# Five equal chunks become seven of two sizes in a one-queue streaming kernel (x + alpha·fx)

## Chip, cores and metric

The kernel runs on 1 core of one Trainium2 chip. The metric is the device time of one execution in microseconds (us), lower is better. The time before is 153.1 us, the median of six runs between 152.75 and 153.47.

## What is computed

```
B, S, D = 512, 32, 640          # x, fx, out: bfloat16 [512, 32, 640]; alpha: bfloat16 [1]
def reference(x, fx, alpha):
    return x + alpha * fx
```

Each of the three large arrays holds 10,485,760 elements, 20.97 MB. The kernel reads two of them and writes one, 62.92 MB in all, and does one multiply and one add for each element.

## The kernel before

The arrays are seen as 128 rows, one for each partition, of 81,920 elements (160 KiB) that lie contiguously in memory. Each row is cut into five chunks of CHUNK = 16,384 elements (32 KiB), so that a load or a store of one chunk is 128 rows of 32 KiB, 4 MiB.

There are two pools of buffers on the chip: `xs` with four buffers for chunks of x (line 54) and `fs` with two for chunks of fx (line 55). Chunk k goes through four steps:

- `load_x(k)` (line 59) and `load_f(k)` (line 63) are DMAs from memory into a buffer of each pool.
- `compute(k)` (line 69) is one instruction of the vector engine (DVE), scalar_tensor_tensor, which writes fx·alpha + x over the x buffer. For the last chunk it is cut into two halves.
- `store(k)` (line 80) is a DMA from the x buffer to the output; for the last chunk there are two, one for each half.

All of these DMAs are issued by one engine, SyncE (SP; its sequencer is SPq in the profile), into one DMA queue (q1). SP issues in the order of the program and waits ahead of an instruction whose buffer is not free or whose data is not there. The order is written by hand (`manual_schedule`, lines 85 to 105). On SP's queue, with s for a store, it reads

```
x0 f0 x1 f1 x2 | f2 s0 x3 | f3 s1 x4 | f4 s2 | s3 | s4a s4b
```

What holds back an issue is of three kinds. A load of fx into a used buffer waits until the compute that read it is done: f2 waits for compute 0, f3 for compute 1, f4 for compute 2. A load of x into a used buffer waits until the store out of it has landed: x4 waits for s0. A store waits for its compute. The 16 DMA engines of the core take the DMAs of the queue in order, eight rows of each DMA to an engine.

The scalar alpha takes a separate way (`alpha_to_lanes`, lines 16 to 27): a small DMA from the scalar engine's queue, a 1x128 matmul that copies the value to all partitions, and a copy to a_f. It is done 2.3 us into the span.

Of the kernel before, what the change touches and what calls it, by code (L numbers as in the profile page):

```python
# [1 line left out]

# [4 lines left out]

ACT = mybir.ActivationFunctionType
ALU = mybir.AluOpType
F32 = mybir.dt.float32  # L10
BF16 = mybir.dt.bfloat16

CHUNK = 16384


def alpha_to_lanes(nc, consts, psum, alpha, eng):

    P = nc.NUM_PARTITIONS
    a_1 = consts.tile([1, 1], alpha.dtype, name="a_1")
    eng.dma_start(out=a_1[:], in_=alpha[None, :])  # L20
    ones = consts.tile([1, P], alpha.dtype, name="ones")
    nc.vector.memset(ones[:], 1.0)  # L22
    a_ps = psum.tile([P, 1], F32, name="a_ps")
    nc.tensor.matmul(a_ps[:], ones[:], a_1[:], start=True, stop=True)  # L24
    a_f = consts.tile([P, 1], F32, name="a_f")
    nc.vector.tensor_copy(out=a_f[:], in_=a_ps[:])  # L26
    return a_f


@with_exitstack  # L30
def kernel(
    ctx: ExitStack,
    tc: tile.TileContext,
    x: bass.AP,
    fx: bass.AP,
    alpha: bass.AP,
    out: bass.AP,
):
    nc = tc.nc
    P = nc.NUM_PARTITIONS  # L40
    xv = x.flatten_outer_dims().rearrange("(p n) d -> p (n d)", p=P)
    fxv = fx.flatten_outer_dims().rearrange("(p n) d -> p (n d)", p=P)
    ov = out.flatten_outer_dims().rearrange("(p n) d -> p (n d)", p=P)
    F = xv.shape[1]
    K = F // CHUNK
    assert K * CHUNK == F and K == 5

    consts = ctx.enter_context(tc.tile_pool(name="consts", bufs=1))
    psum = ctx.enter_context(tc.tile_pool(name="psum", bufs=1, space=bass.MemoryType.PSUM))
    xs = ctx.enter_context(tc.tile_pool(name="xs", bufs=4))  # L50
    fs = ctx.enter_context(tc.tile_pool(name="fs", bufs=2))
    ctx.enter_context(tc.manual_schedule())

    a_f = alpha_to_lanes(nc, consts, psum, alpha, nc.scalar)
    xt, ft = {}, {}

    def load_x(k):
        xt[k] = xs.tile([P, CHUNK], x.dtype, tag="x", name="x_t")
        nc.sync.dma_start(out=xt[k][:], in_=xv[:, bass.ts(k, CHUNK)])  # L59

    def load_f(k):
        ft[k] = fs.tile([P, CHUNK], fx.dtype, tag="f", name="f_t")
        nc.sync.dma_start(out=ft[k][:], in_=fxv[:, bass.ts(k, CHUNK)])

    def compute(k, parts=1):
        n = CHUNK // parts
        for j in range(parts):
            s = bass.ts(j, n)
            nc.vector.scalar_tensor_tensor(  # L69
                out=xt[k][:, s],  # L70
                in0=ft[k][:, s],
                scalar=a_f[:],
                in1=xt[k][:, s],
                op0=ALU.mult,
                op1=ALU.add,
            )

    def store(k, j=0, parts=1):
        n = CHUNK // parts
        nc.sync.dma_start(  # L80
            out=ov[:, k * CHUNK + j * n : k * CHUNK + (j + 1) * n],
            in_=xt[k][:, bass.ts(j, n)],
        )

    load_x(0)
    load_f(0)
    load_x(1)
    load_f(1)
    load_x(2)
    compute(0)  # L90
    load_f(2)
    store(0)
    load_x(3)
    compute(1)
    load_f(3)
    store(1)
    load_x(4)
    compute(2)
    load_f(4)
    store(2)  # L100
    compute(3)
    store(3)
    compute(4, 2)
    store(4, 0, 2)
    store(4, 1, 2)


# [1 line left out]
_INS = ['x', 'fx', 'alpha']  # L109
_OUTS = [((512, 32, 640), 'bfloat16')]  # L110


# [23 lines left out]
```

## Time and profile before

| What | Value |
|---|---|
| Median of six runs | 153.1 us (152.75 to 153.47) |
| The profiled execution's own time | 153.15 us |
| Its span, first to last instruction | 151.4 us |
| DVE busy | 86.9 us (57%) in 8 instructions |
| DMA queue q1 | 62.92 MB, busy 97.6% of 16 engines' span |
| Mean DMA rate over the span | 416 GB/s |

The profile tells for each engine how long it was busy and what ended its idle time; for DMAs, when SP issued one and how long after it landed. A DMA has landed when the last of its 16 engines has posted its completion. In this execution the DMAs of q1 were issued and landed at these times (us from the span's start):

| DMA | x0 | f0 | x1 | f1 | x2 | f2 | s0 | x3 |
|---|---|---|---|---|---|---|---|---|
| issued | 0.7 | 1.2 | 1.6 | 2.1 | 2.7 | 40.3 | 40.7 | 41.1 |
| landed | 13.14 | 22.85 | 32.56 | 42.28 | 52.00 | 62.28 | 72.21 | 81.93 |

| DMA | f3 | s1 | x4 | f4 | s2 | s3 | s4a | s4b |
|---|---|---|---|---|---|---|---|---|
| issued | 59.7 | 60.1 | 72.3 | 79.7 | 80.1 | 109.4 | 130.4 | 139.1 |
| landed | 91.98 | 101.73 | 111.40 | 121.45 | 131.14 | 140.82 | 145.68 | 150.53 |

s4a and s4b are 2 MiB each (128 rows of 16 KiB), all others 4 MiB.

The trace also records each row that a DMA engine moved, as a packet with its start and duration. In this execution a row of 32 KiB took 1,213 ns in the median, and a row of 16 KiB 611 ns.

### The profile page before, as it was taken

How to read it: one execution, taken by the hardware profiler on the slowest of the kernel's cores; microseconds unless marked ns; L12 is line 12 of the kernel's file. 1: busy time of each engine (PE TensorE's matmuls, PEld its weight loads, DVE VectorE, ACT ScalarE, POOL GpSimd, SP SyncE). 2: the span in 40 equal slices, each digit the busy share in tenths (PEclk: the TensorE clock that was granted, in tenths of full speed). 3: DMA queues.
4: the chain of work that ended last, by engine and by line, in shares of the span. 5: the costliest groups of instructions: out<-in, count | busy, mean ns of one | idle time of the engine just before them, and what ended most of it. 6: DMA issues, size and time to landing. Idle time of an engine off the chain costs nothing.

```text
span 151.4 us, 85 instructions
## 1 busy us (share of the span) xinstructions
PE 0.2 (0%) x1; PEld 0.1 (0%) x1; DVE 86.9 (57%) x8; POOL 0.2 (0%) x4
## 2 busy tenths in 40 slices
PE   0000000000000000000000000000000000000000
PEld 0000000000000000000000000000000000000000
DVE  0000009999689997599990006999800089997000
POOL 0000000000000000000000000000000000000000
DMA  6999999999999999999999999999999999999993
GB/s 182 459 450 424 424 416 416 433 442 459 450 424 424 416 416 416 407 424 416 416 416 433 476 424 442 433 416 407 424 442 433 459 433 442 416 416 403 437 424 139
DMA packets 2306, 62.92 MB, mean 416 GB/s; under 512 B 258, under 2 KB 258, under 8 KB 258
## 3 DMA queue, kind: packets, MB, share of 16 engines
q1 hardware_dynamic: 2304, 62.92, 97.6%
q10 hardware_dynamic: 2, 0.00, 0.0%
HBM read 41.94 MB, written 20.97 MB: 416 GB/s over the span
## 4 chain that ended last, share of the span: by engine, by line
DMA 56%; DVE 29%; DVEq 6%; issue 0%; SPq 0%
DMA f_t<-in_fx_dram 56%; DVE x_t L69 29%; DVEq L131 6%; SPq L59 0%; DVEq L69 0%
## 5 line engine op out<-in xcount | busy, mean ns | idle before, releaser
L69 DVE SCALAR_TENSOR_TENSOR x_t<-f_t,a_f,x_t 128x16384 bf16<-128x16384 bf16 (+1 forms) x6 | 86.6, 14439 | 50.2 <-DMA f_t<-in_fx_dram 50.2
L26 DVE COPY a_f<-a_ps 128x1 f32<-128x1 f32 x1 | 0.2, 158 | 1.1 <-PE a_ps L24 1.1
L22 DVE MEMSET ones<- 1x128 bf16 x1 | 0.2, 165 | 0.8 <-PEq L120 0.8
L24 PE MATMUL a_ps<-a,ones 1*128 1x1 bf16 x1 | 0.2, 159 | 1.9 <-DMA a<-in_alpha_dram 1.9
L120 POOL MEMSET const-bfloat16-1.0<- 128x1 bf16 x1 | 0.1, 102 | 0.0
L120 POOL MEMSET const-uint8-127<- 128x1 uint8 x1 | 0.1, 102 | 0.0
L24 PEld LDWEIGHTS <-ones 1*128 1x128 bf16 x1 | 0.1, 100 | 1.0 <-DVE ones L22 1.0
L120 POOL MEMSET const-float32-1.0<- 128x1 f32 x1 | 0.1, 99 | 0.0
L120 POOL MEMSET const-float32-0.0<- 128x1 f32 x1 | 0.1, 98 | 0.2 <-issue 0.2
## 6 DMA issues: line engine op xcount, KB each, us to landing
x_t<-in_x_dram SPq DMA_DIRECT2D x5, 4096.0 KB, 35.0
f_t<-in_fx_dram SPq DMA_DIRECT2D x5, 4096.0 KB, 32.3
out_dram<-x_t SPq DMA_DIRECT2D x4, 4096.0 KB, 36.6
out_dram<-x_t SPq DMA_DIRECT2D x2, 2048.0 KB, 15.3
a<-in_alpha_dram ACTq DMA_DIRECT2D x1, 0.0 KB
```

Source lines behind the costliest of these rows:

```text
L22: nc.vector.memset(ones[:], 1.0)
L24: nc.tensor.matmul(a_ps[:], ones[:], a_1[:], start=True, stop=True)
L26: nc.vector.tensor_copy(out=a_f[:], in_=a_ps[:])
L69: nc.vector.scalar_tensor_tensor(out=xt[k][:, s], in0=ft[k][:, s], scalar=a_f[:], in1=xt[k][:, s], op0=ALU.mult, op1=ALU.add,)
L120: nc = _bacc.Bacc("TRN2", target_bir_lowering=False, num_devices=1)
L131: with _tile.TileContext(nc) as tc:
```

## The change

The five equal chunks become seven: four of 8,192 elements (16 KiB rows, 2 MiB for a load or store) and then three of 16,384 (32 KiB rows, 4 MiB). The buffers keep their number and their size of 32 KiB for each partition; a small chunk fills half of one. The last chunk is no longer cut: it is computed by one instruction and stored by one DMA. The order on SP's queue becomes

```
x0 f0 x1 f1 x2 | f2 s0 x3 | f3 s1 x4 | f4 s2 x5 | f5 s3 x6 | f6 s4 | s5 | s6
```

The waits are of the same kinds: f2 to f6 wait for computes 0 to 4, and x4, x5, x6 wait for the landing of s0, s1, s2. There are 21 DMAs on q1 in place of 16 and seven large instructions on DVE in place of six; SP, its one queue and the path of alpha are as before.

```diff
-CHUNK = 16384
+SIZES = [8192, 8192, 8192, 8192, 16384, 16384, 16384]
+STARTS = [sum(SIZES[:k]) for k in range(len(SIZES))]
+SLOT = max(SIZES)
...
+    def cols(k):
+        return slice(STARTS[k], STARTS[k] + SIZES[k])
+
     def load_x(k):
-        xt[k] = xs.tile([P, CHUNK], x.dtype, tag="x", name="x_t")
-        nc.sync.dma_start(out=xt[k][:], in_=xv[:, bass.ts(k, CHUNK)])
+        xt[k] = xs.tile([P, SLOT], x.dtype, tag="x", name="x_t")
+        nc.sync.dma_start(out=xt[k][:, : SIZES[k]], in_=xv[:, cols(k)])
...
-    def compute(k, parts=1):
-        n = CHUNK // parts
-        for j in range(parts):
...
+    def compute(k):
+        c = SIZES[k]
+        nc.vector.scalar_tensor_tensor(
+            out=xt[k][:, :c],
+            in0=ft[k][:, :c],
...
-    def store(k, j=0, parts=1):
...
+    def store(k, eng=nc.sync):
+        eng.dma_start(out=ov[:, cols(k)], in_=xt[k][:, : SIZES[k]])
...
     load_f(2)
     store(0)
     load_x(3)
-    compute(1)
-    load_f(3)
-    store(1)
-    load_x(4)
-    compute(2)
-    load_f(4)
-    store(2)
-    compute(3)
-    store(3)
-    compute(4, 2)
-    store(4, 0, 2)
-    store(4, 1, 2)
+    for k in range(4, len(SIZES)):
+        compute(k - 3)
+        load_f(k - 1)
+        store(k - 3)
+        load_x(k)
+    compute(4)
+    load_f(6)
+    store(4)
+    compute(5)
+    store(5)
+    compute(6)
+    store(6)
```

More of the change, by code (lines that the diff above doesn't have):

```diff
@@ L44 @@
     F = xv.shape[1]
-    K = F // CHUNK
-    assert K * CHUNK == F and K == 5
+    assert sum(SIZES) == F
     consts = ctx.enter_context(tc.tile_pool(name="consts", bufs=1))
@@ L55 @@
     xt, ft = {}, {}
+    def cols(k):
+        return slice(STARTS[k], STARTS[k] + SIZES[k])
     def load_x(k):
-        xt[k] = xs.tile([P, CHUNK], x.dtype, tag="x", name="x_t")
-        nc.sync.dma_start(out=xt[k][:], in_=xv[:, bass.ts(k, CHUNK)])
+        xt[k] = xs.tile([P, SLOT], x.dtype, tag="x", name="x_t")
+        nc.sync.dma_start(out=xt[k][:, : SIZES[k]], in_=xv[:, cols(k)])
     def load_f(k):
-        ft[k] = fs.tile([P, CHUNK], fx.dtype, tag="f", name="f_t")
-        nc.sync.dma_start(out=ft[k][:], in_=fxv[:, bass.ts(k, CHUNK)])
-    def compute(k, parts=1):
-        n = CHUNK // parts
-        for j in range(parts):
[L68 to L76, printed above, removed]
-    def store(k, j=0, parts=1):
[L79 to L82, printed above, removed]
-        )
+        ft[k] = fs.tile([P, SLOT], fx.dtype, tag="f", name="f_t")
+        nc.sync.dma_start(out=ft[k][:, : SIZES[k]], in_=fxv[:, cols(k)])
+    def compute(k):
[3 more added lines that the diff above has]
+            in0=ft[k][:, :c],
+            scalar=a_f[:],
+            in1=xt[k][:, :c],
+            op0=ALU.mult,
+            op1=ALU.add,
+        )
+    def store(k, eng=nc.sync):
+        eng.dma_start(out=ov[:, cols(k)], in_=xt[k][:, : SIZES[k]])
     load_x(0)
```

## Prediction, made before the changed kernel was run

> **What bounds it now.** I read the page's slices first, for the engine that is never idle, then the queues, then the chain that ended last.
>
> ```profile
> DVE  0000009999689997599990006999800089997000
> ...
> DMA  6999999999999999999999999999999999999993
> ...
> q1 hardware_dynamic: 2304, 62.92, 97.6%
> ```
>
> The DMA engines are full in every slice but the first and the last, while DVE is at rest at the start, at the end and three times between. So the time is 62.92 MB through one queue, a start, an end, and the few moments at which the queue goes slower than it can. The chain says "DVE" for long stretches; it has to be read with this in mind:
>
> ```profile
> 40.29 21.98 DMA f_t<-in_fx_dram
> ...
> 62.37 17.30 DVE x_t L69
> ...
> 79.68 41.77 DMA f_t<-in_fx_dram
> ```
>
> A load that is issued at 79.68 and lands 41.77 us later is not slow: it stands behind what is already queued. While DVE computes, that backlog moves. A wait on DVE costs something only if the queue runs empty, and before the change it never does: s4b is issued at 139.1, and s4a ahead of it lands at 145.7.
>
> The queue's pace comes from the landings. The loads x0 to x2 land 9.71 us apart, 4 MiB each; s2 and s3 take 9.69 and 9.68; the halves s4a and s4b 4.86 and 4.85. From the first landing at 13.14 on, 14 units of 4 MiB are left, and 14 x 9.71 = 135.9 would end at 149.1. The last one lands at 150.53, so **1.45 us** are lost in mid-stream. The landings tell where: f2 takes 10.28 and s0 9.93, together 0.80 over (the packets show all 16 engines with two slow rows at 58 to 61 us, 1.3 to 2.0 us each where 1.21 is the median). From s0's landing to f4's there are two phases of loads behind a store: x3 and f3 take 19.77 where 2 x 9.71 = 19.42, and x4 and f4 19.72; that is 0.35 + 0.30 = 0.65 over. Single rows of 1.3 to 1.7 us show at 73.5, 89.4, 102.8 and 118.5 us, all among loads, and none among the stores at the end.
>
> **The change, part by part.** The bytes are the same; start (x0's first row begins 1.0 us after its issue) and end (0.85 us from the last landing to the span's end) stay. Three things can move.
>
> *Does the queue run dry?* I put the new order through the same paces: 9.71 us for 4 MiB, 4.86 for 2 MiB, the first landing at 8.3 (13.14 less one half). DVE starts 0.13 us after a landing (22.85 to 22.98) and takes
>
> ```profile
> L69 DVE SCALAR_TENSOR_TENSOR x_t<-f_t,a_f,x_t 128x16384 bf16<-128x16384 bf16 x4 | 69.1, 17284 | 37.9 <-DMA f_t<-in_fx_dram 37.9
> L69 DVE SCALAR_TENSOR_TENSOR x_t<-f_t,a_f,x_t 128x8192 bf16<-128x8192 bf16 x2 | 17.4, 8749 | 12.3 <-DMA f_t<-in_fx_dram 12.3
> ```
>
> so 8.75 us for a small chunk and 17.28 for a large one; SP issues 0.02 us after that. The rows of the queue move until 0.35 us ahead of a landing (the last row ends at 150.19, its DMA lands at 150.53). The stages in which SP waits:
>
> | waiting DMA | released by | at us | queue has rows until |
> |---|---|---|---|
> | f2, s0, x3 | compute 0: 13.1 to 22.0 | 22.0 | 27.4 (x2) |
> | f3, s1 | compute 1: 23.0 to 31.7 | 31.7 | 41.9 (x3) |
> | x4 | s0 lands | 37.4 | 51.6 (s1) |
> | f4, s2 | compute 2: 32.7 to 41.5 | 41.5 | 61.3 (x4) |
> | x5 | s1 lands | 52.0 | 75.9 (s2) |
> | f5, s3 | compute 3: 47.3 to 56.0 | 56.0 | 85.6 (x5) |
> | x6 | s2 lands | 76.3 | 100.2 (s3) |
> | f6, s4 | compute 4: 71.6 to 88.8 | 88.8 | 109.9 (x6) |
> | s5 | compute 5: 95.8 to 113.1 | 113.1 | 129.3 (s4) |
> | s6 | compute 6: 120.1 to 137.4 | 137.4 | 139.0 (s5) |
>
> Behind a waiting issue stand only DMAs that the queue does not need yet; x5 and x6 each hold up a load of fx behind them, but these wait longer for their computes anyhow. All covers are over 5 us except the last one. There the new kernel computes 16,384 elements in one go, and only s4 and s5 (19.4 us) lie beside landing, start, compute and issue (0.35 + 0.13 + 17.28 + 0.02 = 17.8): **1.6 us** are left. The issue itself needs some of it. No DMA in this trace is issued into a queue about to run dry except x0: its first rows begin 1.0 us after the issue on the first engine and 1.57 on the last. 1.57 is still under 1.6, so I charge nothing. If it did run dry, x0 is again the nearest row: its first rows took up to 2.31 us where 1.21 is usual, so 1.57 + 1.10 - 1.6 = 1.05 us is the other end. The tail is worth 0 to +1.05; I take 0. The Trainium skill bears on this place ("DMA: Bandwidth & Descriptors", section "Latency and other measured facts"): it gives some 0.6 us to the first byte of a hardware-issued DMA, where the row above has 1.0; by the page the cover would be 1.0 us and the tail safe, by the row it is just met.
>
> *More and shorter rows.* Before there are 14 DMAs of 4 MiB and 2 of 2 MiB; after 9 and 12: five full ones become ten halves. Ten DMAs x 8 rows an engine x (611 - 1213/2 = 4.5 ns) = 0.36 us; by the landings, (4.86 + 4.85 - 9.68) x 5 = 0.15. Below nothing is excluded, as no row shows halves cheaper than a whole. I take +0.25. The skill has a rule that speaks against this edit far more strongly (same page, section "Anatomy of one DMA — SWDGE (gpsimd) path"): each DMA costs some 2.0 us besides its bytes, so that five more would be an estimated +10 us. That page's figure is for another way of issuing, and the landings at the end (9.68, 4.86, 4.85) leave no room for it while the queue has work.
>
> *More alternation of loads and stores.* This is the part that decides. Two phases of loads behind a store cost 0.65 before. After the change there are four: x3 f3 behind s0, x4 f4 behind s1, x5 f5 behind s2, x6 f6 behind s3. Priced by phases it is +0.65. Priced by bytes, 16.8 MB of loads behind the first store become 29.4 (4.2 in halves, 25.2 in wholes): 0.65 x 29.4/16.8 = 1.14, so +0.49. The lower end is 0, if the slow rows come by elapsed time. I take +0.55, between the two prices that tie them to loads behind stores, since no slow row shows among the loads before 52 us.
>
> The stall of 0.80 at 58 us I leave where it is. DVE's total, 4 x 8.75 + 3 x 17.28 = 86.8 against 86.6, lies under the DMAs.
>
> **Sum.** 153.15 (this execution's own time; span 151.4 and 1.77 around it; median 153.1) + 0.25 + 0.55 + 0 = **153.95**, 0.55% over the median. About 0.3% (0.46 us) is what a measurement can tell here.
>
> **Rivals.**
>
> 1. *The tail runs dry.* A cover of 1.6 us is the only thin one, and any lag of DVE eats it. If s6 starts as x0 did, 153.95 + 1.05 = 155.0. For it: x0's slow first rows. Against: the slowest engine sets the end, and it is the one with most rows still queued.
> 2. *The other side: slow rows come by time, not by alternation.* They stand 13.4 to 15.9 us apart (73.5, 89.4, 102.8, 118.5, and the stall at 58 would fit in). Then four phases instead of two cost nothing, and 153.15 + 0.25 = 153.4, not slower by what can be told. It decides if the two added phases bring under 0.2 us. Against it: nothing of the kind at 15, 30 or 44 us, nor in the stores after 121.
> 3. *The stall at 58 us belongs to the old order* (the first fx load into a reused buffer, beside compute 1). Then it goes with it: 153.4 - 0.80 = 152.6. For it: it is the largest loss in the stream; against: f2 comes in the same place of the new order too.
>
> That the change would not take effect I exclude: the instruction order of the built kernel has 21 DMAs on SP in the order above and seven computes.
>
> **Chances.** Forecast 0.44 (0.05 of it so small that it counts as no change), tail 0.17, slow rows by time 0.26, stall gone 0.13. Slower by over 0.3%: 0.39 + 0.17 = 0.56; within 0.3%: 0.05 + 0.26 = 0.31; faster: 0.13. The range runs from 152.6 (stall gone) to 155.0 (tail dry at its full price); the mishaps that would add up beyond these ends are left out. The forecast's own range is 153.6 to 154.3 (153.15 with rows at 0.15 to 0.36 and phases at 0.3 to 0.8).
>
> **What would show it.** Right: DMA slices at 9 throughout; s6's first rows at once behind s5's; halves landing 4.85 to 4.9 us apart; each pair of loads behind a store 0.3 us or more over 9.71 a unit. Wrong in the tail: a slice at 8 or less near 139 us, and s6 landing over 9.8 us after s5. Wrong in the alternation: x4 f4, x5 f5 and x6 f6 each at 19.4 us. Wrong altogether: an empty queue in mid-stream, which would mean a wait that I have not seen.

## The result and the profile after

The changed kernel takes **154.61 us** (median of 19 runs, 153.48 to 155.31) against 152.9 us before (38 runs). The ratio is **1.0098, 95% interval 1.0077 to 1.0118**: 1.5 us slower. The forecast was 153.95, slower, in a range of 152.6 to 155.0. In two later sets of runs, each on one chip beside the kernel before, the ratio was 1.0038 (1.0008 to 1.0068) and 1.0078 (1.0049 to 1.0106). The sign is the same three times; the size is not.

The profiled execution took 154.98 us, its span is 153.2. These are the lines of its page that answer to those shown of before, and the row of rates below them:

```profile
DVE  0005979959903990000899960199993089997000
...
DMA  6999999999999999999999999999999999996993
GB/s 188 424 428 441 428 419 436 441 342 415 432 432 436 471 419 419 419 436 398 505 415 419 419 419 406 419 501 419 411 411 428 462 453 436 411 411 291 411 411 145
...
q1 hardware_dynamic: 3024, 62.92, 96.8%
```

A slice is 3.83 us. Two slices stand out: the ninth (30.6 to 34.5 us, 342 GB/s) and the 37th (138 to 142 us, DMA at 6 tenths, 291 GB/s). The second looks like the dry tail that was a rival of the prediction, and it is the largest hole in the picture. The runs below show that it costs nothing. What does cost something can hardly be seen here: it is mostly the work of one engine out of 16, and the rows show the mean.

The chain of waits has the last computes behind loads of fx that land late (start, duration, what):

```profile
42.17 31.07 DMA f_t<-in_fx_dram
...
73.43 17.30 DVE x_t L71
90.73 0.02 issue
90.75 32.38 DMA f_t<-in_fx_dram
...
123.31 17.29 DVE x_t L71
```

f4 lands at 73.24 where the paces in the prediction had 71.4, f6 at 123.12 where they had 120.0. Both the issue and the transfer are in time; it is the last of the 16 engines that is late. The completions of each DMA show it. This table gives the moment at which the first and the last engine were done with a DMA, in the profiled execution after, and the spread between the two:

| DMA | x2 | f2 | f3 | f4 | s2 | x5 | f5 | x6 | f6 | s4 | s5 | s6 |
|---|---|---|---|---|---|---|---|---|---|---|---|---|
| first engine | 27.11 | 32.56 | 47.25 | 71.51 | 76.64 | 86.05 | 96.06 | 110.63 | 120.36 | 130.01 | 139.67 | 151.53 |
| last engine | 27.70 | 33.30 | 48.27 | 73.24 | 78.17 | 87.83 | 98.82 | 113.42 | 123.12 | 132.85 | 142.50 | 152.25 |
| spread | 0.6 | 0.7 | 1.0 | 1.7 | 1.5 | 1.8 | 2.8 | 2.8 | 2.8 | 2.8 | 2.8 | 0.7 |

The spread grows at f3, f4 and f5, the last load ahead of a store each time, and keeps within some 0.3 of its size between, until s6. It does not grow at f6, though s4 follows. In the profile before it ends at 1.5.

The trace does not number the engines, but each row starts within a few ns of the end of the row ahead of it on its engine, so the rows fall into 16 chains. In the changed kernel's profile the engine that ends last owes the growth at f4 and f5 to two single rows: 1.95 us at 70.9 and 2.64 us at 94.7, where 1.21 is the median. From f2 on, all rows that are over 12% slower than the median of their size are among the last three rows of a load ahead of a store, and all but one among the last two. No DMA is issued at 46, 70, 94 and 119 us, where those of f3 to f6 stand, and DVE is idle then, so neither is the cause there.

The same account as in the prediction, with the last landings. All in us over the even pace of 9.71 for 4 MiB and 4.86 for 2 MiB:

| Loss over the even pace | before | after |
|---|---|---|
| loads at the start (after: x0 to x2 land 4.87 to 4.90 apart) | 0.01 | 0.12 |
| first change from loads to a store (f2, s0) | 0.79 | 1.00 |
| loads between stores (before: 0.35 + 0.30; after: 0.13 + 0.63 + 1.23 - 0.07) | 0.65 | 1.92 |
| stores s1 to s3 (after) and the rest | -0.02 | 0.22 |
| **sum** | 1.4 | 3.3 |

The difference is 1.8 us, and the profiled executions differ by as much (153.15 and 154.98). Of it, 1.27 lie in the loads between stores.

### The profile page after: what moved, and what is told of

The parts are those of the page before. It is cut to its first block, busy times and chain, and to the rows that moved or that the text cites. A ratio compares the mean times of both kernels' runs of the same rounds, so it can differ in the third digit from the quotient of the medians.

```text
span 153.2 us, 95 instructions
## 1 busy us (share of the span) xinstructions
PE 0.2 (0%) x1; PEld 0.1 (0%) x1; DVE 87.2 (57%) x9; POOL 0.2 (0%) x4
## 4 chain that ended last, share of the span: by engine, by line
DMA 57%; DVE 34%; issue 0%; SPq 0%; DVEq 0%
DMA f_t<-in_fx_dram 57%; DVE x_t L71 34%; SPq L63 0%; DVEq L71 0%
## 5 line engine op out<-in xcount | busy, mean ns | idle before, releaser
L71 DVE SCALAR_TENSOR_TENSOR x_t<-f_t,a_f,x_t 128x8192 bf16<-128x8192 bf16 (+1 forms) x7 | 86.9, 12408 | 51.5 <-DMA f_t<-in_fx_dram 51.5
```

The lines of the kernel that those rows point to most:

```text
L71: nc.vector.scalar_tensor_tensor(out=xt[k][:, :c], in0=ft[k][:, :c], scalar=a_f[:], in1=xt[k][:, :c], op0=ALU.mult, op1=ALU.add,)
```

## The experiments

Theory A is that of the prediction: the loss lies in the changes of the queue from loads to stores and back. B: it lies in the uncut tail. C: it lies in the number of DMAs and their shorter rows. A later theory, D, makes A sharper: the price of a change is mostly a lag of the slowest engine. Ratios are against the kernel before in the same set of runs; the kernel before has a median of 152.72 us in the set of the cut, the uncut and the paired kernels, 152.73 in that of the halved and the grouped ones, and 153.01 in the last, which has what was run side by side and the best of both.

### The tail

**Changed kernel, last chunk cut.**

```diff
-    compute(6)
-    store(6)
+    compute(6, 2)
+    store(6, 0, 2)
+    store(6, 1, 2)
```

> The changed kernel with its last chunk computed and stored in two halves, nothing else. In the changed kernel's profile 15 of the 16 DMA engines stand empty for about 2 us ahead of the last store, and the slowest one does not. Theory A (the loss of 1.5 us lies in the added changes of the queue from loads to stores and back): the slowest engine sets the end, so 0 to -0.5 us against the changed kernel, ratio to the kernel before 1.006 to 1.010. Theory B (the uncut tail): back near the kernel before, ratio 1.000 to 1.003.

Measured: 153.49 us, ratio 1.0046 (1.0015 to 1.0078). This lies between the two ranges, and the changed kernel was not in this set, so it decides little. It was run again beside the changed kernel, below.

**Kernel before, last chunk uncut.**

```diff
-    compute(4, 2)
-    store(4, 0, 2)
-    store(4, 1, 2)
+    compute(4)
+    store(4)
```

> The kernel before with its last chunk uncut (one compute, one store of 4 MiB); order and sizes else as before. The cover beside the last compute is then the same 1.6 us as in the changed kernel. Theory A: 0 to +0.4 us, ratio 1.000 to 1.003. Theory B (tail): all of the loss, ratio 1.008 to 1.012.

Measured: 152.42 us, ratio 0.9979 (0.9957 to 1.0001), a little under A's range and far from B's. The uncut tail, with the same 1.6 us of cover, costs the kernel before nothing. In its profile the uncut s4 lands 9.67 us behind s3, at full pace.

**Both side by side.** First the changed kernel for the third time:

> The changed kernel again, as the base on the chip of these four runs. Its loss was 0.98% in the first comparison and 0.38% in the second. Theory D (the price of each change from loads to stores is mostly a lag of the slowest DMA engine, which differs from run to run and from chip to chip): anything from 1.003 to 1.012, with runs that scatter over 1.5 us or more and a floor at least 0.3 us over that of the kernel before.

Measured: 154.50 us (152.92 to 155.28), ratio 1.0078. Its lowest run is 0.34 over the lowest of before, and its runs scatter over 2.4 us, all as D has it.

> The changed kernel with the last chunk cut in two, now beside the changed kernel on one chip. Theory A: within 0.3 us of the changed kernel. Theory B (uncut tail): at least 0.6 us faster than it.

Measured: 154.72 us (six runs), ratio 1.0114 (1.0088 to 1.014), 0.2 over the changed kernel's median. B needed 153.9 or less, and the lowest of the six is 154.39. **B falls.** The windows around the hole tell why. The columns that count are the second last, the mean share of the 16 engines that were busy, and the last, GB/s. The changed kernel, from its first profile:

```profile
138.00:139.60 1.60, 0.00 (x0) 0.00 (x0) 1.60 (x1) 0.00 (x0) 1.00 0.81 348
139.60:141.40 1.80, 0.00 (x0) 0.00 (x0) 1.00 (x1) 0.00 (x0) 1.00 0.09 36
141.40:151.50 10.10, 0.00 (x0) 0.00 (x0) 0.00 (x0) 0.00 (x0) 1.00 0.97 415
```

With the last chunk cut, in the last set:

```profile
138.00:139.60 1.60, 0.00 (x0) 0.00 (x0) 1.60 (x1) 0.00 (x0) 1.00 0.95 410
139.60:141.40 1.80, 0.00 (x0) 0.00 (x0) 1.38 (x1) 0.00 (x0) 1.00 0.98 419
141.40:151.50 10.10, 0.00 (x0) 0.00 (x0) 0.00 (x0) 0.00 (x0) 1.00 0.78 336
```

The hole is filled, and what was won there is lost in the row below: 14 engines end by 149.9, and the last one ends at 152.2, no earlier than in the changed kernel (151.9). In the changed kernel 15 engines waited for s6, up to 2.3 us, while the rows of the slowest engine have no gap over 0.02 us. Its s5 landed at 142.50 and its s6 at 152.25, 9.75 later.

### Fewer changes from loads to stores

**Changed kernel, stores in pairs.** The loop is written out here. The end of the order stays, and the 21 DMAs are the same.

```diff
     load_f(2)
-    store(0)
     load_x(3)
     compute(1)
     load_f(3)
+    store(0)
     store(1)
     load_x(4)
     compute(2)
     load_f(4)
-    store(2)
     load_x(5)
     compute(3)
     load_f(5)
+    store(2)
     store(3)
     load_x(6)
```

> The changed kernel's seven chunks with stores in pairs: s0 and s1 behind f3, s2 and s3 behind f5, so that the queue changes from loads to stores three times in place of five. Chunk sizes, rows and the uncut tail stay. Theory A: two changes fewer at 0.5 to 0.75 us each, ratio to the kernel before 1.000 to 1.004. Theory B (tail) and theory C (21 DMAs with shorter rows): as the changed kernel, ratio 1.008 to 1.012.

Measured: 152.81 us, ratio 1.0005 (0.9984 to 1.0027).

> Stores in pairs and the last chunk cut in two, on the changed kernel's seven chunks. Theory A: as with the pairs alone or up to 0.3 us less, ratio 0.999 to 1.003. Theory B: 1.000. Theory C (rows and number of DMAs): still 1.006 or more, since 22 DMAs are left.

Measured: 152.74 us, ratio 0.9999 (0.9979 to 1.002). Pairs take the loss back; the cut adds nothing to that. In this set the kernel with the cut tail alone had 153.49: the two have the same DMAs and the same cut and differ in the order alone, by 0.75 us.

> The changed kernel with stores in pairs (three changes from loads to stores in place of five), beside the changed kernel on one chip. Theory A: it takes back nearly all of the loss that the changed kernel shows here, and ends within 0.3 us of the kernel before. Theories B and C: as the changed kernel.

Measured, beside the changed kernel's 154.50: **152.76 us**, ratio 0.9992 (0.9973 to 1.0011). Moving two stores gives back the whole loss, with the same chunks, the same DMAs and the same tail. C and B explain none of it. In this profile the spread of the engines goes from 0.4 at the first loads to 0.9 at s5, in the changed kernel beside it from 0.6 to 3.2. The chain:

```profile
32.42 20.27 DMA out_dram<-x_t
...
53.56 42.77 DMA out_dram<-x_t
96.33 0.02 issue
...
96.78 23.91 DMA f_t<-in_fx_dram
...
120.88 17.29 DVE x_t L71
```

f6 lands at 120.69 here, 2.5 us ahead of the changed kernel's in the same set (123.22), and every later step is that much earlier. The chain now goes through stores, since x6 waits for s2; but the queue does not run dry by that. Its line is the first here, that of the changed kernel beside it the second:

```profile
q1 hardware_dynamic: 3024, 62.92, 98.0%
q1 hardware_dynamic: 3024, 62.92, 96.7%
```

**Kernel before, s0 and s1 together behind f3.**

```diff
     load_f(2)
-    store(0)
     load_x(3)
     compute(1)
     load_f(3)
+    store(0)
     store(1)
     load_x(4)
```

> The kernel before with s0 and s1 moved together behind f3, so that the queue changes from loads to stores twice in place of three times; sizes and the cut tail as before. Theory A: one change less, -0.3 to -0.8 us, ratio 0.995 to 0.998. Theories B and C: ratio 1.000.

Measured: 152.39 us, ratio 0.9969 (0.9947 to 0.9991), as A has it. The row of rates of this profile, in slices of 3.76 us, also bears on what the stall at 58 us was:

```profile
GB/s 227 445 419 436 427 419 419 419 427 471 453 436 427 436 419 419 419 419 419 462 453 340 419 419 436 480 436 453 419 427 419 419 419 419 462 453 397 427 419 214
```

The dip (340 GB/s) now stands at 79 to 83 us. The first store of this order begins at 81, that of the changed kernel at 32 (dip at 30.6 to 34.5), that of the kernel before at 61 (slow rows at 58 to 61). In the windows of the kernel before it is the last number, GB/s, that counts:

```profile
52.00:57.00 5.00, 0.00 (x0) 0.00 (x0) 5.00 (x1) 0.00 (x0) 1.00 1.03 446
57.00:62.00 5.00, 0.00 (x0) 0.00 (x0) 2.66 (x1) 0.00 (x0) 1.00 1.07 393
```

In these three kernels it is the price of the first change from loads to a store, and it goes where that change goes. It does not belong to f2. The last kernel below shows that it is not paid always.

### Rows and the number of DMAs

**Kernel before, each 4 MiB DMA as two of 2 MiB** (`H = CHUNK // 2`; the computes and the order stay):

```diff
-        nc.sync.dma_start(out=xt[k][:], in_=xv[:, bass.ts(k, CHUNK)])
+        for j in halves:
+            nc.sync.dma_start(out=xt[k][:, bass.ts(j, H)], in_=xv[:, bass.ts(2 * k + j, H)])
...
-    store(0)
+    store(0, 0, 2)
+    store(0, 1, 2)
```

> The kernel before with each of its 4 MiB DMAs issued as two of 2 MiB, one behind the other: 30 DMAs and 16 KiB rows throughout, the order of loads and stores and the computes unchanged. Theory A (loss in the changes of the queue from loads to stores and back): only the price of shorter rows, 14 x 0.03 to 0.07 us = +0.4 to +1.0, ratio 1.003 to 1.007. Theory C (number of DMAs and short rows make the loss of the changed kernel, 1.5 us for five split ones): 14/5 of it, +4 us, ratio 1.02 or more.

Measured: 152.46 us (152.34 to 152.68), ratio **0.9976** (0.9964 to 0.9988). No theory had this: 30 DMAs with 16 KiB rows are faster than 16. The price per half is there (x0's two halves land 4.89 apart, where half of 9.71 is 4.855), but the spread of the engines stays between 0.3 and 0.5 from the first DMA to the last, and the 12 runs scatter over 0.34 us where the 35 of the kernel before scatter over 1.95. C falls with its sign reversed.

**The same DMAs, half stores between half loads:**

```diff
-    load_f(2)
-    store(0, 0, 2)
-    store(0, 1, 2)
+    load_f(2, (0,))
+    store(0, 0, 2)
+    load_f(2, (1,))
+    store(0, 1, 2)
```

and so for f3 with s1 and f4 with s2.

> The same 30 DMAs as in the kernel with halved DMAs, but with the first half of s0, s1 and s2 put between the halves of f2, f3 and f4: three more changes from loads to stores and three more back, bytes and rows the same. Theory A: 3 x 0.4 to 0.8 = +1.2 to +2.4 us over the halved kernel. Theory C: the same time as the halved kernel within 0.3 us.

Measured: 153.26 us (152.65 to 154.71), ratio 1.0044 (1.0014 to 1.0074). Over the halved kernel that is 0.8 us by the medians, 1.04 by the ratios: A's sign, with less than its size; three added changes cost 0.3 us each. The scatter goes from 0.34 to 2.06 us. The order alone does that, with DMAs, rows and bytes unchanged.

### The changed kernel again, and the best of both

> The changed kernel once more, on the chip of these runs, as the base for the comparison: ratio 1.008 to 1.012, and a second profile. Theory A: excess over 9.71 us for 4 MiB among loads ahead of a store again, above all in f2, f4 and f5, though of other sizes. If the slow rows came by elapsed time they would stand elsewhere than ahead of the stores.

Measured: 153.41 us (152.73 to 154.68), ratio 1.0038, below what was expected. This profile (153.11 us) is of a mild execution: the spread ends at 1.1 where the first profile had 2.8, and f6 lands at 121.28. It is 1.87 us shorter than the first one, and 1.7 of that is the difference in spread. The slow rows stand ahead of s0, s2 and s3 again (30 to 32, 70 and 94 us), where the first profile has them. In the paired kernel, whose stores stand elsewhere, the rows at these times are not slow; most of its slow rows stand at 40 to 41, 89 and 118 to 119 us, ahead of its s0, s2 and s4.

**Both edits that gained,** s0 and s1 behind f3 and each DMA in halves, on the kernel before:

> The kernel before with both edits that gained: s0 and s1 together behind f3 (two changes from loads to stores in place of three) and each DMA as two of 2 MiB. Theory A with the rows' price at nothing or below: ratio 0.994 to 0.998, scatter under 0.5 us. If the halves and the grouping save the same lag, it is no faster than either alone, 0.997.

Measured: **152.33 us** (152.18 to 152.93), ratio **0.9955** (0.9936 to 0.9974), the fastest kernel of its set by its median. The scatter, 0.75 us, is over the 0.5 expected, and as the grouped and the halved kernel ran in another set, with ratios of 0.9969 and 0.9976, it is not shown that both edits together beat either one. The rates have no dip:

```profile
GB/s 152 431 453 422 427 422 435 444 427 422 427 418 431 431 444 427 422 422 422 435 431 440 422 427 422 435 444 431 427 418 431 422 448 431 427 422 427 448 431 218
```

Between the first and the last slice the lowest is 418. The spread of the engines is 0.6 throughout.

## Why the prediction was right, and where it was off

The sign was right in all three comparisons, and so was the mechanism behind it. That the time of 154.61 lies in the stated range of 152.6 to 155.0 is in part luck: it lies above the forecast's own range of 153.6 to 154.3, and the rest of the way up was put there for a dry tail, which cost nothing.

*The queue as the bound, and no empty queue in mid-stream.* Right. f2 was issued at 21.9, x5 at 53.2 and f6 at 90.8, within 2 us of the table, and s6 at 140.6, later by 3.2 with the lag that f6 had by then. No cover but the last was used up.

*The tail at 0.* Right, but by a narrower way than I had it. I named two signs of a dry tail: a slice at 8 or less near 139 us, and s6 over 9.8 us after s5. The first came and the second did not (9.75). The first is a mean over 16 engines, and I had not asked which of them would be empty: 15 were, the one that ends last was not. Rival 1 had this in its "against". The first rows of s6 began 0.8 us after the issue, a little under x0's 1.0.

*More and shorter rows at +0.25.* This step failed in its bound. "Below nothing is excluded, as no row shows halves cheaper than a whole" looked at the pace of single rows alone. The halved kernel is faster by 0.24%. In its profile the halves cost 0.3 us more than the kernel before from x0's landing to x2's, and save 0.7 us from s0's to f4's, where the slowest engines fall behind in the kernel before. The pace of single rows could not show that; it is read from one profile of each kernel.

*More alternation at +0.55.* That alternation costs time was right and decided the sign: the pairs take back the whole loss, the added changes in the halved kernel cost 0.8 to 1.0, the grouped kernel gains 0.3%. **The size is the term that was too small: 1.27 us instead of 0.55** in the profiled execution. Both prices, by phases and by bytes, took the cost to be even. The four phases measured 0.13, 0.63, 1.23 and -0.07 us, so that two of the four miss the 0.3 us named as the sign of being right, and the slow rows stand at the end of a phase and not all over its bytes. In the mild profile of the same kernel f4 and f5 added only 0.2 and 0.1 to the spread. The price is mostly a lag that one engine takes on at a change and keeps to the end. Two phases of one execution were too few to see that it scatters.

*The stall of 0.80, left where it is.* It stayed about as large (1.00) but not in its place: it went with the first store to 30 us. The prediction has two slow rows there on all 16 engines; the rows show the last one slow on all 16 and the one ahead of it on 14. Rival 3, that it belonged to the old order and goes with it, falls. Rival 2, slow rows by elapsed time, falls with the places of the slow rows, which move with the stores.

What stays open: why a change from loads to stores slows the last rows ahead of it, and why mostly one engine; why the lag is large in some executions and small in others; and why halves cost nothing at the first change in the grouped and halved kernel while the seven-chunk kernels, with 16 KiB rows there too, pay 0.5 to 1.5. Only the rates and the lags were shown, not their cause.

## What to carry to other kernels

Where one queue is full all the time, its order can still have a price, here up to 1.1% (154.50 against 152.76 us): put loads together and stores together as far as the buffers allow, and count how often the queue changes from loads to stores. A DMA is done when its last engine is done, so read the spread between first and last completion along the stream before believing a mean; a hole in that mean costs nothing if the slowest engine has none. And price a lag from several executions, since one profile shows one draw of it.

## What the runs showed that I had not expected

- The last two rows of most engines ahead of the first store are slow: in the changed kernel mostly 0.8 to 1.2 us where 0.61 is the median; in the kernel before 1.3 to 2.0 where 1.21 is.
- One engine can fall behind the others by some 2 us in two changes (f4, f5), by one row of 1.9 to 2.7 us at each, and keep that lag for the rest of the stream; in the changed kernel's first and third profile the spread ends at 2.8 and 3.2 us, in its second at 1.1.
- DMAs of 2 MiB in place of 4 MiB, in the order of the kernel before, held the spread at 0.5 us and the scatter of the time at 0.34 us; the same DMAs with three more changes scatter over 2.06 us.
